# A linear-attention and SwiGLU block on one core: order of the start-up loads, of VectorE's first features, of the transposes and of the weight loads

## The chip, the cores and the metric

The kernel runs on one core of a Trainium2 chip. TensorE multiplies matrices into PSUM (8 banks of 128x512 f32), ScalarE and VectorE read PSUM and SBUF, GpSimd (POOL) works in SBUF, SyncE (SP) only issues DMAs, and ScalarE (ACT) issues a few as well. The engines run their own instruction streams in order and wait for each other by semaphores. The metric is the device time of one execution in microseconds.

## The reference

The input x has 2048 rows of 512 columns. It is normalised row by row, and the result feeds two branches that are added to x:

```python
x = A_x
xn = _layernorm(x, axis=-1)
# linear attention, 32 heads of 16 columns
q, k, v = xn @ wqkv                      # split into heads
phi = lambda t: where(t > 0, t + 1, exp(t)) + 1e-6
kv = einsum("bhsd,bhse->bhde", phi(k), v)
z = einsum("bhsd->bhd", phi(k))
o = (phi(q) @ kv) / (phi(q) . z + 1e-6)
A = o @ wo
# SwiGLU, 1792 hidden columns
B = (silu(xn @ w_gate) * (xn @ w_up)) @ w_down
return x + A + B
```

## The kernel before, in words

The 2048 rows are 16 tiles of 128 (`t`), and in the second half 4 chunks of 512 (`C`). A planner class keeps one list per engine in the order of the Python calls; it derives the waits from named resources (a bank, a tile's `xn`, a piece of weights). So the order on each engine is the order in which the program is written.

The first half runs over the 16 tiles. For each tile VectorE takes the statistics (`stat`: `bns` and `agg`, lines 277 to 281, then `rstd_pow`, line 293, in which GpSimd computes the reciprocal root) and the normalised tile (`xn_dve`, line 283). The tile must be transposed for the matmuls. Tiles 0 to 3 go through TensorE and a ScalarE copy (`transpose_half`, `transpose_pe`, lines 308 and 336), the others through a DMA transpose that SP issues right behind `xn` (`transpose_dma`, line 354; `xn`, line 475). TensorE then multiplies with K's and Q's weights (`kproj`, `qproj`, 4 matmuls of 512 columns each, line 366) into one of two pairs of banks: K of tile t in bank 0 or 2, Q in bank 1 or 3. ScalarE takes the exponentials (`exp_k`, line 402, `exp_q`), VectorE builds K's features (`feat_k`: `clip`, line 419, and `maxadd`, line 428). The K bank is free again when `maxadd` is done. GpSimd adds the features up for z (`zsum`). `gtacc` (line 461) multiplies the normalised tile with K's features into banks 4 to 7, where it is summed over all 16 tiles; in tile t's turn it is called for tile t-2. The tables `STAT` and `XN` say in whose turn the statistics and the normalisation of later tiles are made.

The loads at the start are split over two queues. SP issues x 0, x 2, half of K's weights, x 3, one piece of Q's weights and x 4; ScalarE issues x 1, half of K's weights, half of Q's weights, another piece of them, and x 5. The loads of x 6 to 15 stand behind these on SP and wait until all of Q's weights have landed. In tile 9's turn SP issues the gate and up weights of the second half, in eight pieces of 128 rows, then V's and the output weights.

The second half runs over 56 steps `j` (4 chunks of 14 blocks of 128 hidden columns). Each step multiplies with the gate weights and the up weights (line 567, 4 matmuls each), ScalarE takes the silu, VectorE the product. Between the steps stand the small attention products, the normalisation by z, and from the second chunk on the output tiles (lines 739 and 750). The down weights are issued by SP behind two transposes for z.

Of the kernel before, what the change touches and what calls it, by code (L numbers as in the profile page):

```python
# [10 lines left out]
P = 128  # L11
S = 2048
D = 512
F = 1792
# [94 lines left out]
def bass_parallel_sum__linear_attn_block__swiglu_ffn__prompt_kernel(  # L109
# [16 lines left out]
    with contextlib.ExitStack() as es:  # L126
# [58 lines left out]
        def bk(i):  # L185
            return ("bank", i)
# [5 lines left out]
        def xload(eng, h, t0, n, after=()):  # L192
            K.dma(
                eng, lambda: h.dma_start(x_sb[:, t0:t0 + n, :], xv[:, t0:t0 + n, :]),  # L194
                r=list(after), w=[("x", t0 + i) for i in range(n)],
            )

        def wqkv_load(eng, h, name, i, c0, n):
            K.dma(
                eng,  # L200
                lambda: h.dma_start(  # L201
                    wqkv_sb[:, c0:c0 + n, i * D:(i + 1) * D],
                    A_wqkv[c0 * P:(c0 + n) * P, i * D:(i + 1) * D].rearrange("(c p) f -> p c f", p=P),
                ),
                w=[(name, c0)],
            )

        def wload(eng, h, name, dst, src):
            K.dma(eng, lambda: h.dma_start(dst[:, :, :], src.rearrange("(c p) f -> p c f", p=P)), w=[(name,)])

        def wpiece(name, dst, src, c):
            K.dma("sp", lambda: sp.dma_start(dst[:, c, :], src[c * P:(c + 1) * P, :]), w=[(name, c)])

        K.op("pool", lambda: pool.memset(warm[:, :], 0.0), w=[("warm",)])
        K.op("act", lambda: act.activation(warm[:, :], warm[:, :], ACT.Exp), r=[("warm",)], w=[("warm",)])
# [3 lines left out]
        wqkv_load("act", act, "wk", 1, 0, 2)  # L219
        wqkv_load("sp", sp, "wk", 1, 2, 2)  # L220
        wqkv_load("act", act, "wq", 0, 0, 2)
        xload("sp", sp, 3, 1)
        wqkv_load("act", act, "wq", 0, 2, 1)
        wqkv_load("sp", sp, "wq", 0, 3, 1)
        xload("sp", sp, 4, 1)
        xload("act", act, 5, 1)
        xload("sp", sp, 6, 4, [("wq", 0), ("wq", 2), ("wq", 3)])
# [63 lines left out]
            )  # L291

        def rstd_pow(t):
            eng, h = ("dve", dve) if t == 0 else ("pool", pool)
            K.op(
                eng,
                lambda: h.tensor_scalar(
                    out=vpe[:, t:t + 1], in0=mv[:, t, 1:2], scalar1=1e-5, scalar2=None, op0=ALU.add,
                ),
                r=[("mv", t)], w=[("vpe", t)],  # L300
            )
            K.op(
                "pool",
                lambda: pool.tensor_tensor(out=rstd[:, t:t + 1], in0=vpe[:, t:t + 1], in1=nhalf[:, :], op=ALU.pow),
                r=[("vpe", t), ("nhalf",)], w=[("rstd", t)],
            )

        def transpose_pe(t, b):
            tb = banks[b].bitcast(bf)[:, 0:512].rearrange("p (c s) -> p c s", c=NDC)
            K.op(  # L310
                "pe",
                [
                    (lambda c=c: pe.transpose(tb[:, c, :], xn_sb[:, t, c * P:(c + 1) * P], ident[:, :]))  # L313
                    for c in range(NDC)
                ],
                r=[("xn", t), ("ident",)], w=[bk(b)],
            )
            K.op(
                "act",
                lambda: act.activation(xnT[:, :, t * P:(t + 1) * P], tb, ACT.Copy),  # L320
                r=[bk(b)], w=[("xnT", t)],
            )
# [52 lines left out]
        def proj_half(t, b, lo, wname, h):  # L375
            K.op(
                "pe",
                [
                    (lambda c=c: pe.matmul(  # L379
                        banks[b], xnT[:, c, t * P:(t + 1) * P], wqkv_sb[:, c, lo:lo + D],  # L380
                        start=(c == 0), stop=(c == NDC - 1),
                    ))
                    for c in (2 * h, 2 * h + 1)
                ],
                r=[("xnTh", t, h), (wname, 2 * h)] + ([(wname, 3)] if wname == "wq" and h else []), w=[bk(b)],
            )

        def kb(t):
            return 2 * (t % 2)
# [4 lines left out]
        def kproj(t):  # L394
            proj(t, kb(t), D, "wk")

        def qproj(t):
            proj(t, qb(t), 0, "wq")

        def exp_k(t):  # L400
            K.op(
                "act", lambda: act.activation(ek[:, t % NE, :], banks[kb(t)], ACT.Exp),  # L402
                r=[bk(kb(t))], w=[("ek", t % NE)],
            )

        def exp_q(t):
            K.op(
                "act", lambda: act.activation(eq[:, t, :], banks[qb(t)], ACT.Exp),
                r=[bk(qb(t))], w=[("eq", t)],
            )  # L410
            K.op(
                "act", lambda: act.activation(pkq[:, t, 1, :], banks[qb(t)], ACT.Copy),
                r=[bk(qb(t))], w=[("pq", t)],
            )
# [19 lines left out]
        def feat_k(t):  # L434
            e = t % NE
            clip(ek[:, e, :], ("ek", e))
            if t >= 2:
                zsum(t - 2, e)
            maxadd(pkq[:, t, 0, :], banks[kb(t)], ek[:, e, :], [bk(kb(t)), ("ek", e)], [("pk", t)])
# [5 lines left out]
        def zsum(t, e):  # L445
            pk = pkq[:, t, 0, :]
            after = [] if e is None else [("ek", e)]
            if t == 0:
                K.op("pool", lambda: pool.tensor_copy(zacc[:, :], pk), r=[("pk", t)] + after, w=[("zacc",)])
            else:  # L450
                K.op(
                    "pool",
                    lambda: pool.tensor_tensor(out=zacc[:, :], in0=zacc[:, :], in1=pk, op=ALU.add),  # L453
                    r=[("pk", t), ("zacc",)] + after, w=[("zacc",)],
                )

        def gtacc(t):
            K.op(
                "pe",
                [  # L460
                    (lambda c=c: pe.matmul(  # L461
                        banks[4 + c], xn_sb[:, t, c * P:(c + 1) * P], pkq[:, t, 0, :],
                        start=(t == 0), stop=(t == NT - 1),
                    ))
                    for c in range(NDC)
                ],
                r=[("xn", t), ("pk", t)], w=[bk(4 + c) for c in range(NDC)],
            )

        def stat(t):  # L470
            bns(t)
            agg(t)
            rstd_pow(t)

        def xn(t):
            xn_dve(t)
            if t >= 4:
                transpose_dma(t)

        stat(0)  # L480
# [4 lines left out]
        xn_dve(1)  # L485
        agg(2)
        rstd_pow(2)
        stat(3)
        xn_dve(2)
        stat(4)  # L490

        fill(8, 512)
        fill(6, P, [("mv", 0)])
# [3 lines left out]
        fill(4, P)  # L497
        proj_half(0, kb(0), D, "wk", 0)
        proj_half(0, kb(0), D, "wk", 1)
        transpose_pe(1, 6)  # L500
        exp_k(0)
        proj_half(0, qb(0), 0, "wq", 0)
        proj_half(0, qb(0), 0, "wq", 1)
        exp_q(0)
# [2 lines left out]
        qproj(1)  # L507
        exp_k(1)
        exp_q(1)
        feat_k(0)  # L510
        xn(3)
        xn(4)
        stat(5)
        kproj(2)
        transpose_pe(3, 4)
        qproj(2)
        exp_k(2)
        exp_q(2)
        feat_k(1)
        xn(5)  # L520
        stat(6)
        feat_k(2)
        gtacc(0)

        STAT = {2: (7,), 3: (8,), 4: (9, 10), 5: (11,), 6: (12,), 7: (13,), 8: (14, 15)}
        XN = {2: (6,), 3: (7,), 4: (8,), 5: (9, 10), 6: (11,), 7: (12,), 8: (13,), 9: (14, 15)}

        for t in range(2, NT):
            if t >= 3:
                kproj(t)  # L530
                exp_k(t)
                qproj(t)
                exp_q(t)
                feat_k(t)
            for i in STAT.get(t, ()):
                stat(i)
            for i in XN.get(t, ()):
                xn(i)
            if t == 9:
                for c in range(NDC):  # L540
                    wpiece("wg", wg_sb, B_w_gate, c)
                for c in range(NDC):
                    wpiece("wu", wu_sb, B_w_up, c)
                wqkv_load("sp", sp, "wv", 2, 0, 4)
                wload("sp", sp, "wo", wo_sb, A_wo)
            if t == 12:
                masks()
            if t >= 3:
                gtacc(t - 2)
        zsum(NT - 2, None)  # L550
        zsum(NT - 1, None)
        gtacc(NT - 2)
# [9 lines left out]
        def ffn_mm(j, w_sb, wname, b):  # L562
            C, fc = j // NFC, j % NFC
            K.op(
                "pe",
                [
                    (lambda c=c: pe.matmul(  # L567
                        banks[b], w_sb[:, c, fc * P:(fc + 1) * P], xnT[:, c, C * 512:(C + 1) * 512],
                        start=(c == 0), stop=(c == NDC - 1),
                    ))  # L570
                    for c in range(NDC)
                ],
                r=[(wname, c) for c in range(NDC)] + [("xnT", 4 * C + i) for i in range(4)], w=[bk(b)],
            )

        def ffn(j):
# [208 lines left out]
            gt_evac(c)  # L785
        z_split()
        z_cols()
        wload("sp", sp, "wd", wd_sb, B_w_down)
        NORM0 = 9
        PE_OUT = {3: 0, 6: 1, 9: 2, 12: 3}  # L790
# [55 lines left out]
```

## Time and profile before

Three runs of the kernel took 213.25, 213.66 and 213.23 us. The profiled execution is a fourth.

| | us |
|---|---|
| median of the three runs | 213.25 |
| lowest and highest | 213.23, 213.66 |
| the profiled execution's own time | 213.49 |
| its span, first to last instruction | 212.3 |
| TensorE busy | 207.1 (98%) |
| VectorE busy | 119.2 (56%) |
| GpSimd busy | 72.7 (34%) |
| ScalarE busy | 68.0 (32%) |

The granted TensorE clock was 1.000 in the whole execution. A line of the timeline reads: start, duration, engine, line of the program, operation, output and inputs, shape, number of instructions; in brackets how long the engine was idle before it and what ended that. A matmul's duration is longer than its share of the stream, since matmuls are pipelined: what one costs is read from the distance of the starts. A line of the waits reads: who waited, for whom, total time, number of times, longest. The answers on DMAs give the time from the start of the issue until the data have landed.

### The profile page before, as it was taken

To read this page: it belongs to the slowest core of one execution; us is meant where nothing else is said; L and a number is where in the kernel's file an instruction comes from. 1 tells how busy PE (TensorE), PEld (TensorE's weight loads), DVE (VectorE), ACT (ScalarE), POOL (GpSimd) and SP (SyncE) were. 2 spreads that over 40 slices of the span, in tenths; PEclk is the share of its full clock that TensorE was granted. 3 is DMA by queue.
4 is the path that set the end of the run, shared out by engine and by line. 5 is a ranking of instruction groups with operands and counts; after the bars stand their busy time and mean duration, and the time that the engine had idled before them with its cause. 6 is when DMAs were issued, how large, how long until landed. Compare 5 with 4: busy or idle time off the path is not lost.

```text
span 212.3 us, 2770 instructions
## 1 busy us (share of the span) xinstructions
PE 207.1 (98%) x985; PEld 96.2 (45%) x1004; DVE 119.2 (56%) x240; ACT 68.0 (32%) x118; POOL 72.7 (34%) x95
## 2 busy tenths in 40 slices
PE   7999999999999999999999999999999999999996
PEld 2444444444544444444444444444444444444454
DVE  3799997333554876546373746464656535374121
ACT  2686666666353332213122302112032213121000
POOL 2548886648021544032130442121414031221100
DMA  5782333897752011110101021102011010110201
GB/s 174 252 216 53 55 70 74 281 388 241 208 173 53 0 25 25 49 27 26 35 16 49 6 31 40 49 0 49 3 49 25 25 25 28 42 33 28 51 28 49
DMA packets 26287, 16.19 MB, mean 76 GB/s; under 512 B 18080, under 2 KB 24864, under 8 KB 26272
## 3 DMA queue, kind: packets, MB, share of 16 engines
q1 hardware_dynamic: 25296, 15.08, 25.8%
q10 hardware_dynamic: 976, 0.92, 1.4%
q8 instruction: 8, 0.13, 0.3%
q14 instruction: 7, 0.06, 0.1%
HBM read 9.70 MB, written 2.10 MB: 56 GB/s over the span
## 4 chain that ended last, share of the span: by engine, by line
PE 94%; DMA 3%; SPq 1%; issue 1%; DVE 1%
PE psum L567 45%; PE psum L750 23%; PE psum L366 12%; PE psum L739 6%; PE psum L461 6%; DMA wqkv_sb<-in_A_wqkv_dram 3%; SPq L194 1%; PE psum L665 0%; PE psum L688 0%; DVE pkq L428 0%; PE psum L379 0%; SPq L201 0%; DVE out_sb L763 0%; DVE ek L419 0%; PE psum L313 0%
## 5 line engine op out<-in xcount | busy, mean ns | idle before, releaser
L582 ACT ACTIVATE sg<-psum 128x512 bf16<-128x512 f32 x56 | 33.4, 598 | 106.9 <-PE psum L567 105.0
L567 PE MATMUL psum<-xnT,wu_sb 128*128 128x512 bf16 x222 | 57.4, 379 | 0.1
L567 PE MATMUL psum<-xnT,wg_sb 128*128 128x512 bf16 x217 | 56.0, 379 | 0.4
L697 POOL TENSOR_TENSOR prod<-pkq,zb 128x512 f32<-128x512 bf16 x16 | 18.6, 1162 | 56.0 <-DVE pkq L428 56.0
L567 PEld LDWEIGHTS psum<-xnT,wu_sb 128*128 128x128 bf16 x224 | 21.9, 98 | 26.5 <-ACT gt_sb L597 0.4
L567 PEld LDWEIGHTS psum<-xnT,wg_sb 128*128 128x128 bf16 x224 | 21.9, 98 | 26.2
L763 DVE TENSOR_TENSOR out_sb<-psum,x_sb 128x512 bf16<-128x512 f32 (+1 forms) x17 | 11.2, 660 | 36.1 <-PE psum L750 36.1
L721 POOL TENSOR_TENSOR pqn<-pkq,rden 128x512 bf16<-128x512 bf16 x16 | 16.9, 1057 | 36.6 <-DVE rden L715 36.6
L588 DVE TENSOR_TENSOR pkq<-psum,sg 128x512 bf16<-128x512 f32 x28 | 19.1, 686 | 18.2 <-PE psum L567 13.6
L366 PE MATMUL psum<-wqkv_sb,xnT 128*128 128x512 bf16 x118 | 28.4, 379 | 0.4 <-DVE pkq L428 0.3
L588 DVE TENSOR_TENSOR xn_sb<-psum,sg 128x512 bf16<-128x512 f32 x28 | 18.8, 671 | 14.2 <-PE psum L567 13.6
L750 PE MATMUL psum<-wd_sb,xn_sb 128*128 128x512 bf16 (+1 forms) x124 | 25.6, 355 | 0.1
L750 PE MATMUL psum<-wd_sb,pkq 128*128 128x512 bf16 x110 | 25.4, 379 | 0.1
L453 POOL TENSOR_TENSOR zacc<-zacc,pkq 128x512 f32<-128x512 f32 x15 | 17.3, 1156 | 7.0 <-DVE ek L419 6.8
L366 PEld LDWEIGHTS psum<-wqkv_sb,xnT 128*128 128x128 bf16 x120 | 11.6, 98 | 14.1 <-ACT xnT L320 0.6
L750 PEld LDWEIGHTS psum<-wd_sb,xn_sb 128*128 128x128 bf16 x126 | 12.3, 98 | 11.9
L750 PEld LDWEIGHTS psum<-wd_sb,pkq 128*128 128x128 bf16 x112 | 11.0, 98 | 13.2
L739 PE MATMUL psum<-m_sb,eq 128*128 128x512 bf16 (+1 forms) x66 | 16.2, 366 | 0.1
L461 PE MATMUL psum<-pkq,xn_sb 128*128 128x512 bf16 x62 | 15.8, 379 | 0.1
L705 DVE TENSOR_REDUCE den<-prod 128x32 f32<-128x512 f32 x16 | 10.9, 684 | 5.9 <-POOL prod L697 5.9
L278 DVE BATCH_NORM_STATS2 stats<-x_sb 128x6 f32<-128x512 bf16 x16 | 10.9, 683 | 4.4 <-DMA x_sb<-in_A_x_dram 4.4
L402 ACT ACTIVATE ek<-psum 128x512 bf16<-128x512 f32 x16 | 9.5, 596 | 8.9 <-DVE pkq L428 3.5
(56 smaller groups left out, 130.6 us busy)
## 6 DMA issues: line engine op xcount, KB each, us to landing
out_dram<-out_sb SPq DMA_DIRECT2D x15, 128.0 KB, 1.7
wg_sb<-in_B_w_gate_dram SPq DMA_DIRECT2D x4, 448.0 KB, 5.5
wu_sb<-in_B_w_up_dram SPq DMA_DIRECT2D x4, 448.0 KB, 9.0
wd_sb<-in_B_w_down_dram SPq DMA_DIRECT2D x1, 1792.0 KB, 7.9
x_sb<-in_A_x_dram SPq DMA_DIRECT2D x2, 512.0 KB, 4.4
x_sb<-in_A_x_dram SPq DMA_DIRECT2D x4, 128.0 KB, 4.3
wqkv_sb<-in_A_wqkv_dram ACTq DMA_DIRECT2D x2, 256.0 KB, 5.2
wqkv_sb<-in_A_wqkv_dram SPq DMA_DIRECT2D x1, 512.0 KB, 10.5
```

The lines of the kernel that those rows point to most:

```text
L278: K.op("dve", lambda: dve.bn_stats(stats[:, t, :], x_sb[:, t, :]), r=[("x", t)], w=[("st", t)])
L366: (lambda c=c: pe.matmul(banks[b], xnT[:, c, t * P:(t + 1) * P], wqkv_sb[:, c, lo:lo + D], start=(c == 0), stop=(c == NDC - 1),))
L453: lambda: pool.tensor_tensor(out=zacc[:, :], in0=zacc[:, :], in1=pk, op=ALU.add),
L461: (lambda c=c: pe.matmul(banks[4 + c], xn_sb[:, t, c * P:(c + 1) * P], pkq[:, t, 0, :], start=(t == 0), stop=(t == NT - 1),))
L567: (lambda c=c: pe.matmul(banks[b], w_sb[:, c, fc * P:(fc + 1) * P], xnT[:, c, C * 512:(C + 1) * 512], start=(c == 0), stop=(c == NDC - 1),))
L582: lambda: act.activation(sg[:, j % NSG, :], banks[gb], ACT.Silu),
L588: lambda: dve.tensor_tensor(out=hT(C, fc), in0=banks[ub], in1=sg[:, j % NSG, :], op=ALU.mult,),
L697: lambda: pool.tensor_tensor(out=p, in0=pkq[:, t, 1, :], in1=zb[:, :], op=ALU.mult),
L721: lambda: pool.tensor_tensor(out=pqn[:, t % NPN, :].rearrange("p (h e) -> p h e", e=DH), in0=pkq[:, t, 1, :].rearrange("p (h e) -> p h e", ...
L739: (lambda g=g: pe.matmul(dst, pqnT(t)[:, g, :], m_sb[:, g, lo:hi], start=(g == 0), stop=False,))
L750: (lambda fc=fc: pe.matmul(dst, hT(C, fc)[:, jj * P:(jj + 1) * P], wd_sb[:, fc, lo:hi], start=False, stop=(fc == NFC - 1),))
L763: lambda: dve.tensor_tensor(out=o, in0=src, in1=x_sb[:, t, lo:hi], op=ALU.add),
```

## The change

It does these things:

- In the loads, two pieces of Q's weights swap their queues, and both stand ahead of x 3.
- VectorE instead of GpSimd adds the epsilon for tile 2's reciprocal root.
- Tile 3 is transposed by DMA instead of by TensorE and ScalarE.
- Tile 3's statistics are made after tile 2's normalisation, and tile 0's features come between them and ahead of tile 4's statistics. `exp_k(0)` comes ahead of the copy of tile 1's transpose on ScalarE.
- `gtacc(1)` runs ahead of tile 3's projections, and up to tile 10 `gtacc` is called for tile t-1; tile 11's turn has none, and from tile 12 on it is t-2 again.
- Statistics and normalisation of tiles 6 to 15 move to later turns.
- The gate and up weights are loaded in halves of the columns, `whalf`, instead of pieces of rows, in tile 10's turn instead of tile 9's. The second half of the gate weights stands behind the output weights, the second half of the up weights behind the transposes for z.

```diff
+        FH = F // 2
+        def whalf(name, dst, src, h):
+            K.dma(
+                "sp",
+                lambda: sp.dma_start(
+                    dst[:, :, h * FH:(h + 1) * FH],
+                    src[:, h * FH:(h + 1) * FH].rearrange("(c p) f -> p c f", p=P),
+                ),
+                w=[(name, h)],
+            )
...
         wqkv_load("act", act, "wq", 0, 0, 2)
+        wqkv_load("sp", sp, "wq", 0, 2, 1)
+        wqkv_load("act", act, "wq", 0, 3, 1)
         xload("sp", sp, 3, 1)
-        wqkv_load("act", act, "wq", 0, 2, 1)
-        wqkv_load("sp", sp, "wq", 0, 3, 1)
         xload("sp", sp, 4, 1)
...
-            eng, h = ("dve", dve) if t == 0 else ("pool", pool)
+            eng, h = ("dve", dve) if t in (0, 2) else ("pool", pool)
...
             xn_dve(t)
-            if t >= 4:
+            if t >= 3:
                 transpose_dma(t)
...
         rstd_pow(2)
-        stat(3)
         xn_dve(2)
-        stat(4)
+        bns(3)
...
+        exp_k(0)
         transpose_pe(1, 6)
-        exp_k(0)
...
         exp_q(1)
-        feat_k(0)
+        clip(ek[:, 0, :], ("ek", 0))
+        agg(3)
+        rstd_pow(3)
+        maxadd(pkq[:, 0, 0, :], banks[kb(0)], ek[:, 0, :], [bk(kb(0)), ("ek", 0)], [("pk", 0)])
+        bns(4)
         xn(3)
-        xn(4)
-        stat(5)
+        agg(4)
+        rstd_pow(4)
         kproj(2)
-        transpose_pe(3, 4)
         qproj(2)
         exp_k(2)
         exp_q(2)
         feat_k(1)
+        xn(4)
+        stat(5)
+        feat_k(2)
         xn(5)
         stat(6)
-        feat_k(2)
         gtacc(0)
+        gtacc(1)
-        STAT = {2: (7,), 3: (8,), 4: (9, 10), 5: (11,), 6: (12,), 7: (13,), 8: (14, 15)}
-        XN = {2: (6,), 3: (7,), 4: (8,), 5: (9, 10), 6: (11,), 7: (12,), 8: (13,), 9: (14, 15)}
+        STAT = {3: (7,), 4: (8,), 5: (9,), 6: (10,), 7: (11, 12), 8: (13,), 9: (14, 15)}
+        XN = {3: (6,), 4: (7,), 5: (8,), 6: (9,), 7: (10,), 8: (11, 12), 9: (13,), 10: (14, 15)}
...
-            if t == 9:
-                for c in range(NDC):
-                    wpiece("wg", wg_sb, B_w_gate, c)
-                for c in range(NDC):
-                    wpiece("wu", wu_sb, B_w_up, c)
+            if t == 10:
+                whalf("wg", wg_sb, B_w_gate, 0)
+                whalf("wu", wu_sb, B_w_up, 0)
                 wqkv_load("sp", sp, "wv", 2, 0, 4)
                 wload("sp", sp, "wo", wo_sb, A_wo)
+                whalf("wg", wg_sb, B_w_gate, 1)
             if t == 12:
                 masks()
-            if t >= 3:
+            if t >= 12:
                 gtacc(t - 2)
+            elif t < 11:
+                gtacc(t - 1)
...
-                r=[(wname, c) for c in range(NDC)] + [("xnT", 4 * C + i) for i in range(4)], w=[bk(b)],
+                r=[(wname, fc // (NFC // 2))] + [("xnT", 4 * C + i) for i in range(4)], w=[bk(b)],
...
         z_cols()
+        whalf("wu", wu_sb, B_w_up, 1)
         wload("sp", sp, "wd", wd_sb, B_w_down)
```

More of the change, by code (lines that the diff above doesn't have):

```diff
@@ L209, in wload @@
             K.dma(eng, lambda: h.dma_start(dst[:, :, :], src.rearrange("(c p) f -> p c f", p=P)), w=[(name,)])
-        def wpiece(name, dst, src, c):
-            K.dma("sp", lambda: sp.dma_start(dst[:, c, :], src[c * P:(c + 1) * P, :]), w=[(name, c)])
+        FH = F // 2
[8 more added lines that the diff above has]
+            )
         K.op("pool", lambda: pool.memset(warm[:, :], 0.0), w=[("warm",)])
@@ L519, in bass_parallel_sum__linear_attn_block__swiglu_ffn__prompt_kernel @@
         feat_k(1)
+        xn(4)
+        stat(5)
+        feat_k(2)
         xn(5)
         stat(6)
-        feat_k(2)
         gtacc(0)
-        STAT = {2: (7,), 3: (8,), 4: (9, 10), 5: (11,), 6: (12,), 7: (13,), 8: (14, 15)}
-        XN = {2: (6,), 3: (7,), 4: (8,), 5: (9, 10), 6: (11,), 7: (12,), 8: (13,), 9: (14, 15)}
-        for t in range(2, NT):
-            if t >= 3:
[L530 to L538, printed above, removed]
-            if t == 9:
-                for c in range(NDC):
-                    wpiece("wg", wg_sb, B_w_gate, c)
-                for c in range(NDC):
-                    wpiece("wu", wu_sb, B_w_up, c)
+        gtacc(1)
+        STAT = {3: (7,), 4: (8,), 5: (9,), 6: (10,), 7: (11, 12), 8: (13,), 9: (14, 15)}
+        XN = {3: (6,), 4: (7,), 5: (8,), 6: (9,), 7: (10,), 8: (11, 12), 9: (13,), 10: (14, 15)}
+        for t in range(3, NT):
+            kproj(t)
+            exp_k(t)
+            qproj(t)
+            exp_q(t)
+            feat_k(t)
+            for f, tiles in ((xn, XN), (stat, STAT)) if t < 0 else ((stat, STAT), (xn, XN)):
+                for i in tiles.get(t, ()):
+                    f(i)
+            if t == 10:
+                whalf("wg", wg_sb, B_w_gate, 0)
+                whalf("wu", wu_sb, B_w_up, 0)
                 wqkv_load("sp", sp, "wv", 2, 0, 4)
                 wload("sp", sp, "wo", wo_sb, A_wo)
+                whalf("wg", wg_sb, B_w_gate, 1)
             if t == 12:
                 masks()
-            if t >= 3:
+            if t >= 12:
                 gtacc(t - 2)
+            elif t < 11:
+                gtacc(t - 1)
         zsum(NT - 2, None)
```

## The prediction

> **What bounds the kernel now.** I read the table of engines first, then the chain of work that ended last, then the waits, and last the timelines of the first 17 us engine by engine. Table and waits (two views):
>
> ```profile
> PE 207.1 (98%) x985; PEld 96.2 (45%) x1004; DVE 119.2 (56%) x240; ACT 68.0 (32%) x118; POOL 72.7 (34%) x95
> ```
> ```profile
> PEld psum L379 <- DMA wqkv_sb<-in_A_wqkv_dram: 0.7, 1, 0.7
> ...
> PE psum L366 <- DVE pkq L428: 0.3, 1, 0.3
> ```
>
> TensorE is the bound, and after start-up it hardly waits: one wait for Q's weights, one for VectorE's features. The chain says where:
>
> ```profile
> 2.70 5.58 DMA wqkv_sb<-in_A_wqkv_dram
> 8.29 0.14 issue
> 8.42 0.59 PE psum L379 x2
> ...
> 10.24 0.70 DVE pkq L428
> 10.95 0.14 issue
> 11.08 1.02 PE psum L366 x4
> ```
>
> The last piece of Q's weights lands at 8.28, 0.14 later TensorE goes on; the next stop is kproj(2), which needs bank 0 back from tile 0's features (done 10.94). From 11.08 on TensorE's timeline has no gap:
>
> ```profile
> 11.08 1.02 PE L366 MATMUL psum<-wqkv_sb,xnT 128*128 128x512 bf16 x4 [0.33 <-DVE pkq L428]
> 11.94 0.39 PE L313 MATMUL psum<-ident,xn_sb 128*128 128x128 bf16 x4
> 12.17 1.03 PE L366 MATMUL psum<-wqkv_sb,xnT 128*128 128x512 bf16 x4
> 13.03 1.03 PE L461 MATMUL psum<-pkq,xn_sb 128*128 128x512 bf16 x4
> 13.89 1.89 PE L366 MATMUL psum<-wqkv_sb,xnT 128*128 128x512 bf16 x8
> ```
>
> Four 512-column matmuls cost 13.89-13.03 = 0.863 us, tile 3's four transposes 12.17-11.94 = 0.22, one tile (K, Q, GT) 2.59. As the stream is full, what the change gains or loses up to kproj(3) stays to the end. The transfer that matters is tile 4's transpose, the first by DMA. The first answer is that transpose alone, the second all twelve, the third the last load of x (tiles 12 to 15):
>
> ```profile
> L357 SPq DMA_TRANSPOSE xnT<-xn_sb x1: 1298/1298/1298, 11.6 to 11.6; - x1
> ...
> DMA to landing us min/median/max: 3.9/3.9/3.9
> ```
> ```profile
> DMA to landing us min/median/max: 2.4/2.5/4.0
> ```
> ```profile
> L194 SPq DMA_DIRECT2D x_sb<-in_A_x_dram x1: 433/433/433, 9.2 to 9.2; - x1
> ...
> DMA to landing us min/median/max: 5.5/5.5/5.5
> ```
>
> So the usual transpose lands 2.5 us after its issue, but tile 4's took 3.87. By the trace's packet and landing records it was issued at 11.61, its packets ran from 12.94 to 14.85, and it landed at 15.47; the last load of x had its last packet at 14.39 and landed at 14.71. The transpose's last packet came 0.46 after that of x.
>
> **Q's weights ahead of x 3.** Piece 2 takes x 3's slot on SP (landed 7.66), piece 3 takes piece 2's on ACT (landed 7.93), x 3 takes piece 3's (8.29). All are 128 KB. So Q's second half starts at 7.93+0.14 = 8.07 instead of 8.42 and ends at 8.50. Bounds: 7.66 and 8.28 (nothing gained). The loads of x 6 to 15, which wait on SP for these pieces, start 0.35 earlier too, and everything behind them on SP.
>
> **exp_k(0) ahead of tile 1's copy on ScalarE.** kproj(0) ends at 7.49, so exp_k(0) runs 7.53 to 8.12, and the copy starts 0.49 after it (the spacing of the two in ScalarE's rows, 7.75 and 8.24), at 8.02, ends 8.62 and releases kproj(1) at 8.75 (hop 0.14, as behind the first copy). That is 0.10 before the old 8.85; of the 0.35 gained, 0.25 is lost here. Then transposes(2) at 9.62 and qproj(1) at 9.84 to 10.70; copy(2) 10.04 to 10.64; kproj(2) at 10.77.
>
> **Tile 0's features ahead of tile 4's statistics.** VectorE: bns(3) starts at 8.31 with x 3 and takes 0.69; clip(0) 9.00; agg(3) 9.18; maxadd(0) 9.28 to 9.97 (before: 10.94). Bank 0 is free long before 10.77, so kproj(2) waits for the copy alone. **Gain 11.08-10.77 = 0.31**; 0.14 if the weights gain nothing; no more than 0.31, as the copy then decides. rstd's add for tile 2 on VectorE (0.15) and xn(2) at about 7.8 hide: its transposes run at 9.62.
>
> **Tile 3 by DMA transpose.** Four TensorE transposes go: **gain 0.22**, and a ScalarE copy (0.60, off the path). With gtacc(1) now ahead of kproj(3), TensorE reaches kproj(3) at 10.77+4x0.863 = 14.22. For xn(3): bns(4) 9.89, xn(3) 10.58 to 10.99 (rstd(3) from POOL is there at about 10.3), issue on SP 11.02. Two rows price the transpose. By the median 2.5 it lands at 13.5: no wait. By tile 4's row it is held behind the loads of x: these end 0.35 earlier, so it lands at 15.47-0.35 = 15.12 (by its own duration, 11.02+3.87 = 14.89; with no earlier loads, 15.47). I take 15.12: the loads are the same, and still in flight when its packets can start (11.02+1.3). Then kproj(3) starts at 15.25: **loss 15.25-14.22 = 1.03** (0 to 1.39). Behind the waiting matmul stand qproj(3), gtacc(2) and all later tiles on TensorE; exp_k(3) on ScalarE waits for it, then VectorE's features of tile 3, then xn(6) and its transpose, all later by the same amount, so no second loss follows. On SP the new transpose stands ahead of tile 4's: that is issued at 12.49 with xn(4) (12.06 to 12.46, behind feat_k(1)), 0.17 after the new one's 1.3 us of issue, and lands by about 16, due at K(4) = 17.84; the loads of x stand ahead of both and are not held.
>
> Here the Trainium skill speaks against the edit: "DMA: Bandwidth & Descriptors", section "Queues, rings and completion order", says that descriptors on one engine are consumed in ring order, whichever instruction is urgent. By that rule the wait is the 1.03 above, by the median row nothing, and tile 4's row sides with the rule.
>
> **GT one tile behind.** From kproj(t) at K: exp_k done K+1.75, clip and maxadd done K+2.8, due at gtacc K+4.3: 1.5 to spare, so zero; without it each tile would pay the excess. In the tiles with two statistics VectorE falls at most 1.1 behind (tiles 7 to 10). xn and transposes go one tile later: tile 6's lands at K(3)+6.4 of 7.77; the tightest is tile 10's (two statistics ahead): issued K(7)+4.76, landing +7.25, due +7.63: 0.4 to spare. Zero, but see the rivals.
>
> **Weights in halves, one tile later.** Before, eight pieces (3584 KB) took 36.25 to 50.07, 259 KB/us, and the last held wu's first matmul back by 0.05 (50.20 for 50.155): **gain 0.05**. After, SP is free of transposes at about 39.6; two halves (1792 KB) land by 48.4, due 49.8 and 50.6. The second wg half stands ahead of z's transposes, which land by 57 (needed about 61), the second wu half by 60 (due 62.8); wd and so z's rows come up to 1 us later, which VectorE feels at the first normaliser, where TensorE has three bank pairs (3.4 us). Cost zero; if these covers were short, the excess.
>
> **Sum:** -0.31-0.22-0.05+1.03 = +0.45. On the profiled execution (213.49, span 212.3 and 1.2 around it): 213.94; on the median 213.25: 213.70. The profiled one lies in the runs' spread (213.23 to 213.66), the mean of all four is 213.41; I say 213.85. A measurement of this kernel tells about 0.2% (0.43) from no change, so this is only just slower.
>
> A second rule of the skill prices what no row here does: "TensorE: Matmul & The Clock Gate", Part 1, halves the clock after an idle window of about 3.4 us. No run shows a gap of 1 us: the longest after the first real matmul is 0.33, at a granted clock of 1.00. By the page a wait of 1.03 keeps the clock.
>
> **Rivals.**
> - The transpose is not held (faster). Its packets slip between those of x, as the median says; it decides if it lands by 14.09, and breaks even at 14.67. For it: tile 4's first packets ran at 12.94, before x had ended. Against: its last ran after. -0.58: 212.91 from the profile, 212.67 from the median.
> - The loads of x end sooner (same). From 11.5 to 12.6 they moved at under half their rate. Without that they end about 0.5 earlier, the wait is 0.5, the sum -0.05: 213.4.
> - A later transpose is late (slower). Tile 10's with 3.9 instead of 2.5 arrives 1.0 late: 214.9. Against: from 20 us on no bulk load is in flight, though one transpose (issued 18.83) took 4.0.
>
> **Chances.** Forecast 0.50 (0.36 over the bound, 0.14 within it), not held 0.24, loads sooner 0.14 (0.12 within, 0.02 faster), later transpose 0.12. So faster 0.26, same 0.26, slower 0.48. The likeliest case's own range is 213.45 to 214.3 (landing 14.9 to 15.5); for 8 in 10 both outer cases are needed: 212.6 to 214.6.
>
> **What would show it.** Right: Q's second half near 8.07, kproj(1) 8.75, kproj(2) 10.77, no ScalarE copy for tile 3, a wait of about 1 us at kproj(3) put down to a DMA transpose landing near 15.1, then no gap until the end. Wrong: kproj(3) at 14.2 without a wait, or waits in tiles 6 to 15, or at the first gate matmul.

## The result and the profile after

Twelve runs of the changed kernel have a median of 214.22 us (213.88 to 215.09), twelve of the kernel before 213.27 us (212.84 to 213.97). The ratio is 1.0047, 95% interval 1.0034 to 1.0061: slower by 0.95 us. The prediction was 0.45 slower (213.85, range 212.6 to 214.6): the direction came, and about twice the size. The profiled execution took 214.42 us, with a span of 213.1. Two executions among the experiments below are no part of the ratios, one of 316.44 us at a granted clock of 0.66 (tile 3 on TensorE again) and one of 1260.3 us (GT two tiles behind, first run).

TensorE is still the bound. From the page, and then from TensorE's waits in the changed kernel (lines have moved: projections are L375 now, the first tile's halves L388):

```profile
PE 208.3 (98%) x1000; PEld 96.0 (45%) x1000; DVE 119.4 (56%) x241; ACT 67.3 (32%) x117; POOL 72.4 (34%) x94
```
```profile
PE psum L375 <- DMA xnT<-xn_sb: 1.1, 1, 1.1
...
PE psum L388 <- DMA wqkv_sb<-in_A_wqkv_dram: 0.3, 1, 0.3
```

The wait for VectorE's features is gone, and a wait for a DMA transpose is there. (The 0.3 is for K's second half, which landed at 7.07.) The chain of the changed kernel shows its place:

```profile
7.84 0.60 ACT ek L411
8.44 0.50 ACT xnT L329
8.93 0.05 issue
8.98 1.04 PE psum L375 x4
...
11.04 4.46 DMA xnT<-xn_sb
15.50 0.14 issue
15.63 1.89 PE psum L375 x8
```

exp_k(0) and behind it the copy of tile 1 release kproj(1), as the prediction had it. Further on the chain runs through tile 3's transpose: issued at 11.04, landed 4.46 us later. TensorE's timeline around the wait, and what the DMA view says of that transpose and of the last two loads of x:

```profile
12.67 1.89 PE L470 MATMUL psum<-pkq,xn_sb 128*128 128x512 bf16 x8
15.63 1.89 PE L375 MATMUL psum<-wqkv_sb,xnT 128*128 128x512 bf16 x8 [1.08 <-DMA xnT<-xn_sb]
```
```profile
L366 SPq DMA_TRANSPOSE xnT<-xn_sb x1: 1297/1297/1297, 11.0 to 11.0; - x1
...
DMA to landing us min/median/max: 4.5/4.5/4.5
```
```profile
L194 SPq DMA_DIRECT2D x_sb<-in_A_x_dram x2: 432/432/433, 8.6 to 9.1; - x2
...
DMA to landing us min/median/max: 4.4/5.1/5.8
```

The eight GT matmuls occupy the stream from 12.67 to 12.67+8x0.216 = 14.40; kproj(3) starts at 15.63. So the wait is 1.24 (the 1.08 in the bracket counts from the modelled end of the last matmul). The last load of x, issued at 9.07, landed at 14.91, and the transpose 0.6 after it. From 15.63 on the chain stays on TensorE to the last output tile, with no other gap.

Against the kernel before: there kproj(3) started at 13.89 with gtacc(1) still to come. With gtacc(1) put ahead of it, as in the changed kernel, it would have started at 13.89+0.863 = 14.75. 15.63 is 0.88 later; the 0.05 at the up weights is won back; together 0.83, and the spans differ by 213.1-212.3 = 0.8. So nothing else of any size moved the end.

### The profile page after: what moved, and what is told of

It reads as the page before. It is cut to its first block, busy times and chain, and to the rows that moved or that the text cites. A ratio compares the mean times of both kernels' runs of the same rounds, so it can differ in the third digit from the quotient of the medians.

```text
span 213.1 us, 2778 instructions
## 1 busy us (share of the span) xinstructions
PE 208.3 (98%) x1000; PEld 96.0 (45%) x1000; DVE 119.4 (56%) x241; ACT 67.3 (32%) x117; POOL 72.4 (34%) x94
## 4 chain that ended last, share of the span: by engine, by line
PE 93%; DMA 5%; ACT 1%; SPq 0%; issue 0%; DVE 0%
PE psum L580 45%; PE psum L763 23%; PE psum L375 11%; PE psum L752 6%; PE psum L470 6%; DMA wqkv_sb<-in_A_wqkv_dram 3%; DMA xnT<-xn_sb 2%; ACT xnT L329 1%; PE psum L678 0%; PE psum L701 0%; SPq L194 0%; ACT ek L411 0%; PE psum L388 0%; DVE out_sb L776 0%; PE psum L322 0%
## 5 line engine op out<-in xcount | busy, mean ns | idle before, releaser
L580 PE MATMUL psum<-xnT,wg_sb 128*128 128x512 bf16 x224 | 57.5, 379 | 0.0
L375 PE MATMUL psum<-wqkv_sb,xnT 128*128 128x512 bf16 x120 | 28.2, 379 | 1.2 <-DMA xnT<-xn_sb 1.1
L601 DVE TENSOR_TENSOR xn_sb<-psum,sg 128x512 bf16<-128x512 f32 x28 | 18.8, 671 | 14.9 <-PE psum L580 14.4
L375 PEld LDWEIGHTS psum<-wqkv_sb,xnT 128*128 128x128 bf16 x120 | 11.5, 98 | 15.7 <-issue 1.7
```

The costliest lines, as they stand in the source:

```text
L375: (lambda c=c: pe.matmul(banks[b], xnT[:, c, t * P:(t + 1) * P], wqkv_sb[:, c, lo:lo + D], start=(c == 0), stop=(c == NDC - 1),))
L580: (lambda c=c: pe.matmul(banks[b], w_sb[:, c, fc * P:(fc + 1) * P], xnT[:, c, C * 512:(C + 1) * 512], start=(c == 0), stop=(c == NDC - 1),))
L601: lambda: dve.tensor_tensor(out=hT(C, fc), in0=banks[ub], in1=sg[:, j % NSG, :], op=ALU.mult,),
```

## The experiments

Theory: tile 3's transpose is held up by the loads of x that stand ahead of it in the DMA queue, and the wait for it is the whole loss. Rivals: a first DMA transpose is slow by itself, or is issued too late; or other parts of the change (features, GT, weights, loads) cost the time. The kernel before was run beside each group: 213.40 us beside the first four runs, 213.20 beside the next four, 213.25 beside the last four.

**Tile 3 on TensorE again.**

```diff
-            if t >= 3:
+            if t >= 4:
                 transpose_dma(t)
...
         kproj(2)
+        transpose_pe(3, 4)
         qproj(2)
```

> The changed kernel with one part undone: tile 3 is transposed by TensorE and copied by ScalarE again. Theory (the whole loss is kproj(3)'s wait of 1.24 us for tile 3's DMA transpose, the other parts gain about 0.2): the wait goes, 0.22 us of transposes come back, so 214.22 - 1.24 + 0.22 = 213.2 us, ratio to before 0.9995, and no gap on TensorE after kproj(2). Rival (the reordered features, GT or the weights cost it): stays at 214.0 to 214.3.

Measured 213.82 us, ratio 1.0007 (0.9989 to 1.0026; the two medians alone give 1.0020). The interval ends below that of the changed kernel, so the loss or most of it is gone, and the other parts together are worth nothing that can be measured. The time is above the 213.2 expected. The profiled execution (214.28) has no wait for a transpose, but K's second half landed at 8.04, and TensorE waited 0.8 for it:

```profile
8.18 0.59 PE L388 MATMUL psum<-wqkv_sb,xnT 128*128 128x512 bf16 x2 [0.76 <-DMA wqkv_sb<-in_A_wqkv_dram]
...
13.86 1.90 PE L470 MATMUL psum<-pkq,xn_sb 128*128 128x512 bf16 x8
15.59 1.89 PE L375 MATMUL psum<-wqkv_sb,xnT 128*128 128x512 bf16 x8
```

**x 12 to 15 behind the transposes of tiles 3 and 4.**

```diff
         xload("sp", sp, 10, 2)
-        xload("sp", sp, 12, 4)
...
         xn(4)
+        xload("sp", sp, 12, 4)
         stat(5)
```

> The changed kernel with the load of x 12 to 15 issued behind the transposes of tiles 3 and 4 on SP. Theory (the transpose is held behind the bulk loads in the DMA queues): tile 3's transpose lands about 13.7, before its due time of 14.3, no wait; 214.22 - 1.24 = 213.0 us, ratio 0.9985 to 0.9990. Rival (a first DMA transpose is slow by itself, or its issue is late): it still takes 3.9 to 4.5 us from issue and the time stays at 214.2.

Measured 213.33 us, ratio 0.9991 (0.9971 to 1.0010): the loss is gone here too, with tile 3 still by DMA. The transpose alone, and TensorE's timeline, in this kernel:

```profile
L365 SPq DMA_TRANSPOSE xnT<-xn_sb x1: 1304/1304/1304, 11.0 to 11.0; - x1
...
DMA to landing us min/median/max: 2.5/2.5/2.5
```
```profile
12.60 1.89 PE L469 MATMUL psum<-pkq,xn_sb 128*128 128x512 bf16 x8
14.32 1.89 PE L374 MATMUL psum<-wqkv_sb,xnT 128*128 128x512 bf16 x8
...
29.00 1.03 PE L469 MATMUL psum<-pkq,xn_sb 128*128 128x512 bf16 x4
30.41 1.89 PE L374 MATMUL psum<-wqkv_sb,xnT 128*128 128x512 bf16 x8 [0.39 <-ACT pkq L420]
```

The same transpose, again the first of the program and issued at the same time, lands in 2.5 us instead of 4.5, and kproj(3) follows GT at 14.32 without a wait. It is neither slow by itself nor late: the loads ahead of it held it up. Whether they do so by the order in the queue or by sharing the DMA engines is not separated: in the changed kernel the first packets of 256 bytes, which are the transpose's, ran at 12.92, while packets of the loads ran until 14.57; here the first ran at 12.25. The time is above the 213.0 expected. In the profiled execution (213.67) 0.55 us went at tile 9: kproj(9) should have started at 29.00+0.86 = 29.86 and started at 30.41. The bracket names ScalarE, which had long been done; tile 9's transpose, issued at 26.00, landed at 30.28, and in the packet records a 16 KB and an 8 KB transfer of the queues that the profile calls instruction run from 26.78 to 29.12.

**512 KB more ahead of the transpose.**

```diff
         xload("sp", sp, 12, 4)
+        K.dma(
+            "sp",
+            lambda: sp.dma_start(wd_sb[:, 0:4, :], B_w_down[0:512, :].rearrange("(c p) f -> p c f", p=P)),
+            w=[("wd",)],
+        )
```

> The changed kernel with 512 KB of the down weights loaded additionally right behind x 12 to 15 on SP, so ahead of tile 3's transpose. (They are loaded again later with the rest.) Theory (queue order): the transpose lands later by what 512 KB take, 1.3 to 1.6 us at 330 to 390 KB per us, and so does everything behind it: 215.5 to 215.8 us. Rival (the transpose is slow by itself, packets of loads and transposes share the engines): landing moves by less than 0.4 us, 214.2 to 214.6.

Measured 219.36 us, ratio 1.0286 (1.0266 to 1.0305): the sign of the theory, but 5.1 us over the changed kernel instead of 1.3 to 1.6. The transpose's landing, TensorE's line, and the granted clock by stretch (PEclk is the column before the DMA share):

```profile
DMA to landing us min/median/max: 7.2/7.2/7.2
```
```profile
18.14 3.57 PE L380 MATMUL psum<-wqkv_sb,xnT 128*128 128x512 bf16 x8 [3.84 <-DMA xnT<-xn_sb]
```
```profile
12.00:18.00 6.00, 2.30 (x11) 0.86 (x9) 3.60 (x9) 1.66 (x4) 2.14 (x5) 0.88 1.26 196
18.00:24.00 6.00, 5.86 (x16) 2.18 (x17) 2.06 (x5) 1.68 (x3) 2.01 (x3) 0.56 0.08 17
24.00:30.00 6.00, 6.00 (x30) 2.69 (x29) 4.13 (x10) 3.80 (x7) 3.60 (x6) 1.00 0.21 44
```

kproj(3) starts at 18.14, 2.51 later than in the changed kernel. That is itself more than the 1.3 to 1.6 expected: x 12 to 15 landed at 15.99 instead of 14.91, the 512 KB at 17.40 and the transpose 0.6 after these, at 18.01. Why the loads took so long is not shown.

The rest, 2.5 us, is the clock. GT's last matmul had its place in the stream until 14.14, so the gap is 4.0 us; in the 6 us from 18 on the granted clock stood at 0.56, and the first twelve matmuls started 0.427 apart instead of 0.216. The Trainium skill, "TensorE: Matmul & The Clock Gate", Part 1, puts the half clock after an idle window of about 3.4 us. That the gap of 4.0 us brought it agrees; but by the trace's clock record the half clock ran from 16.50 to 23.33, so it began when the gap was 2.4 us old. In the profiles with a gap of 2.1 us (two kernels below) matmuls ran 0.216 apart behind it. Yet one other execution of each of these two kernels has a mean clock of 0.992 and took 216.70 and 217.04 us, so a gap near 2 us may not always leave the clock alone. How long it was in these two is not on record, and one execution of the kernel before (215.18 us) shows 0.992 too.

**GT two tiles behind again.**

```diff
         gtacc(0)
-        gtacc(1)
...
-            if t >= 12:
-                gtacc(t - 2)
-            elif t < 11:
-                gtacc(t - 1)
+            gtacc(t - 2)
```

> The changed kernel with GT two tiles behind as in the kernel before (gtacc(1) behind tile 3's projections). Theory (gtacc(1) fills 0.86 us of the wait for tile 3's transpose): the landing stays near 15.5, the wait grows from 1.24 to 2.1 us, 214.22 + 0.86 = 215.1 us. Rival (the place of GT is indifferent, or one tile behind costs): 214.0 to 214.3.

> The changed kernel with GT two tiles behind, once more for its profile: the transpose of tile 3 lands near 15.5 and TensorE's wait ahead of kproj(3) is 2.1 us instead of 1.24 (theory); 1.24 (rival).

Measured 215.37 us (214.90 is the median of the five executions that the ratio counts), ratio 1.0092 (1.0061 to 1.0123), and 215.47 in the second run, a single execution. The profile is the second run's. TensorE there:

```profile
12.69 1.03 PE L470 MATMUL psum<-pkq,xn_sb 128*128 128x512 bf16 x4
15.63 1.89 PE L375 MATMUL psum<-wqkv_sb,xnT 128*128 128x512 bf16 x8 [1.92 <-issue]
```

kproj(3) starts at 15.63 as in the changed kernel, and the wait has grown to 15.63-12.69-0.86 = 2.08. So gtacc(1) ahead of kproj(3) fills 0.86 us of the wait; without it the change would have lost 1.5 to 2 us.

**Tile 3 by DMA alone, on the kernel before.**

```diff
-            if t >= 4:
+            if t >= 3:
                 transpose_dma(t)
...
         kproj(2)
-        transpose_pe(3, 4)
         qproj(2)
```

> The kernel before with one part of the change alone: tile 3 by DMA transpose. Theory (held behind the loads of x): it lands near 15.5, kproj(3), now due at 13.67, starts at about 15.6: 213.4 - 0.22 + 1.94 = 215.1 us. Rival (a transpose off TensorE is a gain, and other parts of the change cost the time): 213.2 us.

Measured 215.05 us, ratio 1.0106 (1.0078 to 1.0134), as the theory says. In its profile the transpose was issued at 10.95 and landed at 15.31; the wait is 15.40-12.47-0.86 = 2.07:

```profile
12.47 1.03 PE L461 MATMUL psum<-pkq,xn_sb 128*128 128x512 bf16 x4
15.40 1.89 PE L366 MATMUL psum<-wqkv_sb,xnT 128*128 128x512 bf16 x8 [1.91 <-issue]
```

**Q's weights first alone, on the kernel before.**

```diff
         wqkv_load("act", act, "wq", 0, 0, 2)
+        wqkv_load("sp", sp, "wq", 0, 2, 1)
+        wqkv_load("act", act, "wq", 0, 3, 1)
         xload("sp", sp, 3, 1)
-        wqkv_load("act", act, "wq", 0, 2, 1)
-        wqkv_load("sp", sp, "wq", 0, 3, 1)
         xload("sp", sp, 4, 1)
```

> The kernel before with the order of the loads alone changed: Q's weights ahead of x 3. Theory (kproj(2) waits for tile 0's features, and these stand on VectorE behind tile 3's statistics, which now wait 0.6 to 0.8 us longer for x 3): kproj(2) 0.3 to 0.5 later, 213.7 to 213.9 us. Rival (TensorE gets its weights earlier and keeps it): 213.0 us. The profile also shows whether K's second half lands later than 6.6 with this order.

Measured 213.76 us, ratio 1.0031 (1.0015 to 1.0047). TensorE no longer waits for Q's weights, but for tile 0's features, since VectorE stands at tile 3's statistics until x 3 is there (VectorE, then TensorE):

```profile
8.29 0.69 DVE L278 BATCH_NORM_STATS2 stats<-x_sb 128x6 f32<-128x512 bf16 x1 [1.35 <-DMA x_sb<-in_A_x_dram]
```
```profile
11.37 1.02 PE L366 MATMUL psum<-wqkv_sb,xnT 128*128 128x512 bf16 x4 [0.55 <-DVE pkq L428]
```

The two edits belong together: the order of the loads alone is a loss of 0.3%, because the features stand behind the statistics that wait for x 3. In the changed kernel the features come first, and no wait for them is left.

**Versions with the loads out of the way.** Three kernels start from the one with x 12 to 15 behind the transposes. The first takes the copy of tile 1 ahead of exp_k(0) again:

```diff
-        exp_k(0)
         transpose_pe(1, 6)
+        exp_k(0)
```

> The kernel with x 12 to 15 behind tile 4's transpose, and tile 1's copy ahead of exp_k(0) on ScalarE again. Theory (the copy, not the weights, releases kproj(1)): kproj(1) and kproj(2) start 0.13 to 0.17 earlier, 213.2 us beside 213.33 for the one without. Rival (kproj(2) is bound by the copy of tile 2 or by the features): no difference.

Measured 212.92 us, ratio 0.9988 (0.9975 to 1.0001). kproj(1) now starts at 9.04, right behind qproj(0) (8.18+4x0.216), so the copy was what released it. The time differs from the 213.33 without this edit by no more than the noise. Tile 9's wait is here again, 0.5 us, its transpose issued at 26.13 and landed at 30.38.

The second leaves exp_k(0) first, and makes statistics and normalisation one turn earlier and GT later:

```diff
         stat(6)
+        stat(7)
+        xn(6)
...
-        STAT = {3: (7,), 4: (8,), 5: (9,), 6: (10,), 7: (11, 12), 8: (13,), 9: (14, 15)}
-        XN = {3: (6,), 4: (7,), 5: (8,), 6: (9,), 7: (10,), 8: (11, 12), 9: (13,), 10: (14, 15)}
+        STAT = {3: (8,), 4: (9,), 5: (10,), 6: (11,), 7: (12,), 8: (13,), 9: (14, 15)}
+        XN = {3: (7,), 4: (8,), 5: (9,), 6: (10,), 7: (11,), 8: (12,), 9: (13,), 10: (14, 15)}
...
-            if t >= 12:
+            if t >= 4:
                 gtacc(t - 2)
-            elif t < 11:
-                gtacc(t - 1)
```

> The kernel with x 12 to 15 behind tile 4's transpose, statistics and normalisation of tiles 6 to 11 one turn earlier again, and GT two tiles behind from tile 4 on. Theory (with x 12 to 15 held, what is left is a late transpose in tiles 6 to 10 whenever another transfer meets it, 0.4 us in the profile of the run without this): no wait on TensorE for any transpose, 212.9 us. Rival (that wait is a chance of one execution): 213.3 us.

Measured 213.48 us, ratio 1.0016 (1.0001 to 1.0031): a miss. Tile 9 no longer waits, but tile 5 does, 0.5 us: GT later brings kproj(5) forward by 0.86, and tile 5's transpose, issued at 15.07, stands behind the load of x 12 to 15, which took from 13.81 to 18.18.

The third has copy 1 first, the earlier turns, GT one tile behind, and x 12 to 15 behind tile 5's transpose (the load stands behind `xn(5)` instead of `xn(4)`).

> The changed kernel with x 12 to 15 behind tile 5's transpose, tile 1's copy ahead of exp_k(0), and statistics and normalisation of tiles 6 to 11 one turn earlier; GT stays one tile behind. Theory (what is left in the run with copy 1 first is 0.4 us at tile 9, whose transpose meets instruction loads): no wait on TensorE for a transpose, 212.5 us, ratio 0.996 to 0.997. Rival (those 0.4 us are chance, or the load of x 12 to 15 now catches tile 6's transpose): 212.9 us or more.

Measured 212.97 us, ratio 0.9994 (0.9969 to 1.0019), runs from 212.52 to 214.78. Its profile (212.84) has no wait on TensorE for any transpose, as expected, but 212.5 was expected, and the time is not below the first version's: the rival's 212.9 or more is what came. Neither is told apart from the kernel before.

**Both kernels once more.**

> The kernel before once more, for when K's second half lands. If its place follows from the change, it is near 6.6 here and near 7.1 in the changed kernel on the same chip; if it is chance or the chip, the two are as far apart as two executions of one kernel. Kproj(2) at 11.1, wait put down to VectorE's features.

> The changed kernel once more: tile 3's transpose lands 0.5 to 0.7 after x 12 to 15, TensorE waits 1.0 to 1.4 us at kproj(3) (theory). K's second half as in the text of the run of the kernel before.

Single executions of 213.06 and 214.40 us on one chip. TensorE in the changed kernel:

```profile
12.26 1.89 PE L470 MATMUL psum<-pkq,xn_sb 128*128 128x512 bf16 x8
15.66 1.89 PE L375 MATMUL psum<-wqkv_sb,xnT 128*128 128x512 bf16 x8 [1.51 <-DMA xnT<-xn_sb]
```

The start went better by 0.41 than in the first profile (GT at 12.26 for 12.67), and kproj(3) did not move: 15.66 for 15.63. In the kernel before kproj(3) started at 13.48 this time, so 14.34 with gtacc(1) behind it: 15.66-14.34 = 1.32 beside a difference of the times of 1.34. The wait is 15.66-12.26-8x0.216 = 1.67 here, more than the 1.0 to 1.4 expected: what is won ahead of it is lost in it.

K's second half landed at 6.14 in the changed kernel and 6.05 in the kernel before in these two, at 7.07 and 6.56 in the first two, and between 5.93 and 8.04 in all traced executions, with the new order of the loads alone at 5.93. The three traced executions with the old order of the loads lie at 6.00 to 6.56, the ten with the new one at 5.93 to 8.04, with a median of 7.0. So the new order need not push it back, but whether it does so on the average is not settled. Where tile 3's transpose is late it does not matter.

## Why the prediction was right, and where its sizes were off

**Direction and place: right.** The forecast was a wait at kproj(3) behind the loads of x, and slower. Undoing the transpose alone, or holding the load alone, removes the loss; the transpose alone makes it.

**The transpose's landing: the term that was mis-sized.** The step "these end 0.35 earlier, so it lands at 15.47-0.35 = 15.12" failed. In the changed kernel the loads of x started 0.15 and 0.24 earlier than in the kernel before (first and second profile), not 0.35, since the last of Q's pieces landed at 8.14 for 8.29 and at 7.85 for 8.10; and they ended no earlier:

| execution | first load of x 6 to 15 issued | last landed | first DMA transpose issued | landed |
|---|---|---|---|---|
| before, first | 8.38 | 14.71 | 11.61 | 15.47 |
| before, again | 8.19 | 14.81 | 11.20 | 15.40 |
| changed, first | 8.23 | 14.91 | 11.04 | 15.50 |
| changed, again | 7.95 | 14.92 | 10.71 | 15.53 |
| changed, GT two behind | 8.32 | 14.92 | 11.15 | 15.55 |
| before, tile 3 by DMA | 8.29 | 14.73 | 10.95 | 15.31 |
| before, Q's weights first | 8.03 | 14.42 | 11.89 | 15.03 |

In every row the transpose lands about 0.6 to 0.8 after the last load, and in all but the last row that lands at 14.7 to 14.9. The upper end that the prediction kept for "no earlier loads", 15.47, is what came. With it the sum is 0.45+0.35 = 0.80 instead of 0.45. With the measured terms it is -0.14 (kproj(2) at 10.94 for 11.08) -0.22-0.05+1.24 = 0.83; the spans differ by 0.8, the medians by 0.95. Why the loads end no earlier was not shown. In the last row they start and end earlier, and the transpose lands at 15.03, near the 15.12 predicted; there the first transpose is issued latest, at 11.89. So a transpose issued earlier may slow the loads, but no run separates this.

**The median row against tile 4's row: right.** 4.5, 4.8 and 4.4 us from issue to landing where the loads are ahead, 2.5 where x 12 to 15 are not. The Trainium skill, "DMA: Bandwidth & Descriptors", section "Queues, rings and completion order", says that descriptors are consumed in ring order on each engine, and the prediction weighed the two rows by it. The landing 0.6 us after the last load agrees with that, though sharing of the engines isn't excluded as the reason.

**exp_k(0) ahead of the copy: right** in its mechanism (the chain shows the two in a row, and copy 1 first frees kproj(1)). kproj(2) came at 10.94 in the first profile and 10.53 in the second, not 10.77: the size hung on when K's second half landed (7.07 and 6.14, for 6.56 in the profile that the prediction read), which the prediction took as fixed. It made no difference to the end, since the wait takes it up.

**Q's weights ahead of x 3: right in kind.** No wait for them is left in the first profile; Q's second half started at 8.29, not 8.07, as kproj(0) had waited for K's second half.

**Features ahead of statistics: right.** xn(3) ended at 11.01 for 10.99 expected, the transpose was issued at 11.04 for 11.02, and maxadd(0) released nothing late.

**GT one tile behind: costless as said.** The prediction counted gtacc(1) in the due time of kproj(3) (14.22), and the run without it shows its worth there, 0.86 us.

**Weights: right.** The first halves landed at 45.7 and 48.4 (expected by 48.4), the second at 54.9 and 59.9, and the 0.05 at the up weights is gone. That 48.4 came is in part luck: the halves were issued from 40.72 on, not from 39.6, and at the 259 KB/us that the prediction names they would have landed at 46.5 by its own start.

**The rivals.** "Not held" is out. "Loads end sooner" did not happen. "A later transpose is late" did not cost the changed kernel anything, but it is real: with x 12 to 15 behind the transposes, tile 9's costs 0.5 us in two profiles, half of the price named. That the changed kernel was spared is chance in the timing of the instruction transfers: in its first profile tile 9's took 3.31 us from 27.31, and TensorE came to kproj(9) only at 31.17. The other gains of the change are real too where that wait is away: kproj(3) starts at 14.32 and 14.19 in the profiles of the first kernel with x 12 to 15 behind the transposes and of the last one, for 14.75, so 0.43 and 0.56 earlier where the prediction has 0.53. The times don't tell it from noise.

## What to carry to other kernels

A transpose moved to a DMA queue had to wait here for what stood in that queue at the time of the issue; read the landing of the nearest such transfer in the same stretch, not the median over the run. A matmul stream that is full hands a wait on to the end undiminished, and the wait takes up whatever was won ahead of it. An order of loads and the order of the engine that consumes them should be looked at together: the order of the loads alone was a loss here (ratio 1.0031); the order of the features alone was not run.

## What the runs showed of the hardware that was not expected

- The loss from a wait on TensorE is not linear: in the profiles a gap of 2.1 us cost 2.1 us, and one of 4.0 us cost another 2.5 us through a granted clock of 0.56 over the next 6 us. The half clock began when that gap was 2.4 us old.
- Transfers of the instruction queues (16 KB and 8 KB) go with late DMA transposes. In 13 profiles (all but that of the first run with GT two tiles behind), 143 transposes of xn had no load in flight ahead of them. The 24 that met such a transfer before they landed took 2.6 to 4.8 us. Of the other 119 all but two took at most 2.53; the two, 2.8 us each, stand right behind a late transpose. No run varied these transfers by themselves. At tile 9 0.5 us of it reached TensorE in two kernels.
- A load of K's weights of 256 KB, issued at 1.72 to 1.73 in all 13, landed anywhere from 5.9 to 8.0 us.
- The warm-up matmuls at the start run at half rate: in the kernel before those of 512 columns start 0.43 apart from 1.22 to 3.35, for 0.216 later. So the granted clock of 1.000 that is given for the whole of that execution does not hold for its first microseconds. Nothing in the argument rests on them.
